# Holding the order of all five engines through the planned slots of a fused attention and mixture-of-experts kernel

## The chip, the cores and the metric

The kernel runs on one core of one Trainium2 chip. The metric is the device time of one launch in microseconds, as the median of three runs. One more execution was taken with the hardware profiler; the views quoted below are of that one.

## The reference, cut to what matters

Windowed attention with four sink positions gives the tokens `x`. A gate picks one of eight experts for each token, and that expert's two-layer network is applied to it.

```python
batch, n_heads, seq, head_dim = (4, 8, 768, 64); n_sink, window = (4, 128)
scores = scale * np.matmul(q, k.transpose(0, 1, 3, 2))
keep = is_sink | in_window
scores = np.where(keep, scores, -1000000000.0)
a = softmax(scores)                       # exp, sum + 1e-9
attn_out = np.matmul(a, v)
x = attn_out.transpose(0, 2, 1, 3).reshape(3072, 512)

logits = x @ w_gate                       # 8 experts
e_idx = np.argmax(logits, axis=1)
for e in range(8):
    mask = e_idx == e
    h = np.maximum(x[mask] @ w1[e], 0.0)  # 512 -> 1024
    ye = h @ w2[e]                        # 1024 -> 512
    out[mask] = gate_w[mask, None] * eom[mask, e, None] * ye
```

## The kernel before, in words

**Two stages.** The first stage runs attention over 16 pairs of heads, writes the tokens to `xd` in DRAM, and routes them. The second stage runs the experts' products over a fixed plan of 17 slots, numbered here k = 0 to 16. Slots 0 to 3 are the experts with most tokens, 256 rows each, known early. Slots 4 to 16 follow `SEQ` and `SIZES`: they hold 6, 1, 6, 2, 4, 1, 4, 2, 4, 1, 4, 2 and 1 units of 64 rows, so their products have m = 3, 3, 2, 2, 2 and 2 tiles of 128 rows, three have m = 1, and four are half tiles of 64 rows. Slot 16 is computed only when a flag asks for it.

**A slot.** "first(k)" is the product with w1 and "second(k)" the product with w2. Slots 0 and 1 use the weights as loaded (`plain1`, `plain2`, L576 and L589), as half slots do (`half1`, `half2`, L676 and L690). The others split each fp32 matrix into two fp32r halves and take three matmuls for one: `mm1_parts` (L545), `single_parts` for m = 1 (L601), `mm2_parts` (L650).

**Weights.** Each matrix comes in four pieces of 512 KB. A piece is loaded into one of four `raw` buffers (L486, on SP's queue), ACT casts it to the high half (L496), and POOL (pieces 0 and 2) or DVE (pieces 1 and 3) subtracts to get the low half (L497). Thirteen places a0 to a3, b0 to b2, c0 to c5 hold the halves; a place comes free when the product that reads it is done. In w1 a piece is one of the four depth blocks, and `mm1_parts` needs all four for its first output block; in w2 a piece serves two of the eight steps f.

**Tokens.** `gather` (L509) issues an indirect DMA on POOL into `xg`. `x_parts` (L519) copies the row factor (L524), transposes on PE (L527), casts on ACT to `xh` (L529) and subtracts on DVE to `xl` (L530), one tile of 128 rows at a time. After each first product `split_relu` (L535) makes `hh` on ACT and `hl` on DVE. `relu_transpose` (L593) is the way for m = 1 and half slots: DVE makes `hr` (L595), PE turns it (L598). `put` (L640) scales on ACT (L642) and scatters with an indirect DMA on POOL (L643).

**What sets the order.** Up to the end of slot 1 everything is emitted inside `tc.manual_schedule` with all five engines (L1060), so each engine runs its instructions as the program writes them. Routing work that is still open ("later": `gate_route`, `final_table`) is emitted in pieces by `points(3)` between the products of slots 0 and 1 (the "lane", L1017). From slot 2 on, only PE is held (the last loop of the second stage); the orders of ACT, DVE, POOL and SP come from the planner, which simulates the program by its own costs. There, weights are asked for up to three products ahead and the planner sets their casts, subtractions and loads where it finds room; the tiles of `x` are transposed in the second half of the product before.

Of the kernel before, what the change touches and what calls it, by code (L numbers as in the profile page):

```python
# [18 lines left out]
P = 128  # L19
# [30 lines left out]
CW = P + 4  # L50


def moe_kernel(tc, qT, kx, vx, vs, wgo, w1, w2, nsink, window, out):
# [7 lines left out]
    with ctx:  # L61
# [400 lines left out]
        def load_weights(which, ereg, slot, whole=False, parts=False):  # L462
# [6 lines left out]
            for i in range(4):  # L469
                view = src[bass.ds(ereg, 1), :, i * kk:(i + 1) * kk, :].rearrange("o p k n -> p (o k) n")  # L470
                if whole:
                    if i % 2 == 0:
                        pool, name = slot()
                    hi = pool.tile([P, kk, n], F32, name=name + "hl"[i % 2])
                    if parts:
                        loads.append(lambda hi=hi, view=view: nc.sync.dma_start(out=hi, in_=view))
                    else:
                        nc.sync.dma_start(out=hi, in_=view)
                    his += [hi[:, j, :] for j in range(kk)]
# [113 lines left out]
        def relu_transpose(mp, ps):  # L593
            hr = mp.tile([P, 4, P], F32, name="hr", bufs=2)
            nc.vector.tensor_scalar(out=hr, in0=ps.rearrange("p (a b) -> p a b", b=P), scalar1=0.0, scalar2=None, op0=ALU.max)  # L595
            tp = ps_t.tile([P, 4, P], F32, name="tp")
# [4 lines left out]
        def single_parts(mp, w, xs, hs):  # L601
# [12 lines left out]
            def turn(q):  # L614
                tp = relu_transpose(mp, both[:, q, :])
# [60 lines left out]
        def half1(mp, w, xf, hs):  # L676
# [28 lines left out]

        mctx = ctx.enter_context(ExitStack())
        ws = {}
        aa, bb, cc = (["%s%d" % (c, i) for i in range(n)] for c, n in (("a", 4), ("b", 3), ("c", NB)))
        second = iter(bb + aa[:1])
# [7 lines left out]
        with ExitStack() as actx:  # L717
# [201 lines left out]
            def early_rank(r):  # L919
                yield from rank_experts(*firsts(r))  # L920
                r0, n = firsts(r)
                for k in range(r0, min(r0 + n, 3)):
                    ws["e%d" % k] = expert_reg(order_i[0:1, k:k + 1])
                    for j in range(2) if k != 1 else ():
                        ws[k, j], loads, splits = load_weights(j, ws["e%d" % k], slot, whole=k == 0, parts=True)
                        if k == 0:
                            behind.extend(loads)
                        else:
                            stream.extend(zip(loads, splits))
                for load, _ in stream[:RAW]:  # L930
                    load()

            def second_weights(j):
                def name():
                    s = next(second)
# [3 lines left out]
            stream, at = [], [0]  # L939

            def weights():
# [429 lines left out]
```

## Time and profile before

| | |
|---|---|
| median of three runs | 574.55 us (572.3 to 582.35) |
| the profiled execution's own time | 581.05 us |
| its span, first to last instruction | 579.3 us |
| mean granted TensorE clock | 0.965 |
| busy: PE, PE weight load | 520.4 us (90%), 393.8 us (68%) |
| busy: DVE, ACT, POOL | 316.8 us (55%), 271.1 us (47%), 308.7 us (53%) |
| HBM read and written | 98.28 MB, 13.45 MB |

Engines: PE is the matmul engine, PEld its weight loads, DVE the vector engine, ACT the scalar engine, POOL GpSimd, SP the queue that issues most DMAs. A row of groups gives line, engine, operation, output and input tiles, shape and count, then total busy time and the mean of one in ns, then the idle time just ahead of the group and what ended it. A row of a timeline gives start, duration, the instruction, and in brackets the wait ahead of it and what ended that wait. A row of windows gives a stretch, its length, the busy time of PE, PEld, DVE, ACT and POOL in it, the granted clock, the DMA engines' busy share and GB/s. In the profiled execution attention ends and the lane begins near 185 us, first(2) starts at 259, the last product ends at 566.

### The profile page before, as it was taken

The numbers are of one execution on the slowest core, as the hardware profiler recorded it, in microseconds if no ns is written. First come the engines' busy times: TensorE is split into PE (matmuls) and PEld (weight loads), VectorE is DVE, ScalarE is ACT, GpSimd is POOL, SyncE is SP. The second block draws the span as 40 slices with busy tenths as digits, with TensorE's granted clock in tenths as the row PEclk, the third lists the DMA queues.
The fourth block names the chain that finished last, engine by engine and source line by source line (L and its number), as shares of the span: only waits on it lengthen the run. The fifth ranks groups of instructions, "written<-read, shape, count | busy, mean of one in ns | idle before, by whom it ended". The sixth has DMA issues, their size and how long they took to land. (4 is left out here: it accounts for less than half of the span.)

```text
span 579.3 us, 10514 instructions
## 1 busy us (share of the span) xinstructions
PE 520.4 (90%) x3432; PEld 393.8 (68%) x3432; DVE 316.8 (55%) x734; ACT 271.1 (47%) x721; POOL 308.7 (53%) x330
## 2 busy tenths in 40 slices
PE   3899999999888979987997999899999899997990
PEld 1566656656565845837896967788777787876870
DVE  5567699698777676982524151342454354553420
ACT  2576666666656122424524254343446354463310
POOL 4557757857856312636626344734466663666210
PEclk9999999999989979997999899999999899998996
DMA  6166776677996986348459645713998739977530
GB/s 228 61 137 185 153 156 166 130 147 209 215 238 102 226 225 165 110 150 286 147 174 360 230 133 193 240 46 126 365 334 270 237 128 320 369 249 242 183 135 19
DMA packets 72498, 112.85 MB, mean 195 GB/s; under 512 B 12044, under 2 KB 38672, under 8 KB 72434
## 3 DMA queue, kind: packets, MB, share of 16 engines
q1 hardware_dynamic: 67970, 98.16, 57.6%
q0 software_dynamic: 4464, 13.91, 6.9%
q8 instruction: 30, 0.49, 0.4%
q14 instruction: 34, 0.28, 0.2%
HBM read 98.28 MB, written 13.45 MB: 193 GB/s over the span
## 5 line engine op out<-in xcount | busy, mean ns | idle before, releaser
L788 ACT ACTIVATE e<-s,nmx 128x132 f32<-128x132 f32 x192 | 69.5, 367 | 66.5 <-DVE nmx L786 55.1
L776 PE MATMUL s<-kr,qr 64*128 64x260 f32 (+1 forms) x384 | 63.2, 429 | 16.2 <-ACT e L788 10.6
L537 DVE SCALAR_TENSOR_TENSOR hl<-s,hh 128x512 fp32r<-128x512 f32 (+1 forms) x32 | 24.0, 755 | 72.2 <-ACT hh L536 72.2
L776 PEld LDWEIGHTS s<-kr,qr 64*128 64x128 f32 x384 | 30.8, 199 | 40.3 <-ACT e L788 29.0
L643 POOL DMA_INDIRECT out_dram<-y,idx x20 | 23.6, 1182 | 48.2 <-ACT y L642 15.4
L536 ACT ACTIVATE hh<-s 128x512 fp32r<-128x512 f32 (+1 forms) x32 | 20.8, 650 | 54.0 <-PE s L556 53.9
L786 DVE TENSOR_REDUCE nmx<-s 128x2 f32<-128x264 f32 x96 | 41.5, 433 | 3.3
L763 POOL TENSOR_SCALAR qr<-qr 128x256 f32<-128x256 f32 x48 | 39.8, 848 | 1.1 <-DMA qr<-in_qT_dram 1.1
L83 POOL TENSOR_SCALAR_AFFINE_SELECT g<-f 128x512 f32<-128x512 f32 (+1 forms) x48 | 28.2, 588 | 21.3 <-DVE f L805 18.7
L788 ACT ACTIVATION_READ_ACCUMULATOR e<-s,nmx 128x1 f32 x192 | 37.6, 196 | 0.0
L782 DVE COPY_PREDICATED s<-maskf,s 128x256 f32<-128x256 int32 x80 | 33.7, 421 | 6.5 <-PE s L776 5.2
L509 POOL DMA_INDIRECT xg<-xd,idx x21 | 27.9, 1327 | 8.8 <-PE tp L527 4.9
L799 PE MATMUL tp<-ident,e 128*128 128x128 f32 x192 | 29.8, 295 | 0.4 <-ACT f L803 0.4
L799 PEld LDWEIGHTS tp<-ident,e 128*128 128x128 f32 x192 | 21.8, 148 | 11.8 <-issue 5.0
L83 POOL TENSOR_SCALAR_AFFINE_SELECT f<-f 128x512 f32<-128x512 f32 (+1 forms) x48 | 27.0, 562 | 3.3
L846 PE MATMUL oA<-f,vt 128*64 128x128 f32 x256 | 26.5, 285 | 0.4
L530 DVE TENSOR_TENSOR xl<-tp,xh 128x512 fp32r<-128x512 f32 x21 | 13.9, 683 | 17.5 <-ACT xh L529 17.5
L274 POOL TENSOR_TENSOR rhs<-oh,ohj 128x512 bf16<-128x512 bf16 x8 | 11.2, 1417 | 21.0 <-DVE oh L265 21.0
L643 POOL DMA_INDIRECT out_dram<-y,idx_e x8 | 8.7, 1084 | 23.7 <-ACT y L642 12.6
L803 ACT COPY f<-tp 128x512 f32<-128x512 f32 x32 | 18.6, 583 | 0.4 <-PE tp L799 0.4
L846 PE MATMUL oA<-g,vt 128*64 128x128 f32 x192 | 18.6, 273 | 0.0
L846 PEld LDWEIGHTS oA<-f,vt 128*64 128x64 f32 x256 | 14.4, 136 | 6.1 <-issue 3.3
(609 smaller groups left out, 1593.3 us busy)
## 6 DMA issues: line engine op xcount, KB each, us to landing
raw<-in_w_dram SPq DMA_DIRECT2D x88, 512.0 KB
kr<-in_kx_dram SPq DMA_DIRECT2D x16, 396.0 KB
qr<-in_qT_dram SPq DMA_DIRECT2D x16, 384.0 KB
vt<-in_vx_dram SPq DMA_DIRECT2D x16, 384.0 KB
xd<-x SPq DMA_DIRECT2D x16, 384.0 KB
a0h<-in_w_dram SPq DMA_DIRECT2D x4, 512.0 KB
a0l<-in_w_dram SPq DMA_DIRECT2D x4, 512.0 KB
b0h<-in_w_dram SPq DMA_DIRECT2D x3, 512.0 KB
```

Source lines behind the costliest of these rows:

```text
L83: nc.gpsimd.affine_select(out=ap, in_=ap if src is None else src, pattern=pattern, compare_op=op, fill=fill, base=base, channel_multiplier=cm)
L509: nc.gpsimd.indirect_dma_start(out=xg, out_offset=None, in_=xd[0:n + 1, :], in_offset=bass.IndirectOffsetOnAxis(ap=ids[0], axis=0))
L536: nc.scalar.activation(out=hi, in_=ps, func=AF.Relu)
L537: nc.vector.scalar_tensor_tensor(out=lo, in0=ps, scalar=0.0, in1=hi.bitcast(F32), op0=ALU.max, op1=ALU.subtract)
L643: nc.gpsimd.indirect_dma_start(out=where, out_offset=bass.IndirectOffsetOnAxis(ap=ids, axis=0), in_=y, in_offset=None, bounds_check=rows - ...
L763: nc.gpsimd.tensor_scalar(out=q, in0=q, scalar1=SCALE, scalar2=None, op0=ALU.mult)
L776: nc.tensor.matmul(out=s[:, a, o0:P + CW], lhsT=z["q"][r, t * P:(t + 1) * P], rhs=z["k"][r, k0:k0 + P + CW - o0], start=True, stop=True)
L782: nc.vector.copy_predicated(out=both[:, :, 4:CW], mask=bc(maski[:, 1, 4:CW], 1, 2), data=s[:, :, 0:P])
L786: nc.vector.tensor_reduce(out=m, in_=both, axis=AX.X, op=ALU.max, negate=True)
L788: nc.scalar.activation(out=z["e"][:, t, a, :], in_=both[:, a, :], func=AF.Exp, bias=m[:, a:a + 1], scale=1.0, accum_out=z["rs"][:, t, a:a ...
L799: nc.tensor.transpose(out=tp[:, k, :], in_=z["e"][:, 2 * j + k // 2, k % 2, 4:CW], identity=ident)
L846: nc.tensor.matmul(out=o, lhsT=v[:, kt, r], rhs=src[:, kt, a, :], start=t == kt == 0 or t == kt + 1 == 4, stop=False, skip_group_check=True)
```

## The change

All of the second stage moves into the region in which every engine is held. The routing pieces and slots 0 to 15 become one lane, each of whose steps is a piece of a product with a cost in microseconds; a running clock `now` adds these costs up, and `free` notes when a place comes free by that clock.

After each step `supply` may set one more piece of weights into the program: a split (cast and subtraction, followed by the next raw load), or for a half slot a load straight into its place. It does so when the place has been free for `LAG`, when `PACE` has passed since the last one, and when the raw load was issued at least `LAND` ago, all by `now`. `ensure` sets whatever is still missing directly ahead of the product that needs it.

The transposes of the next slot's `x` are set by the same clock, some microseconds ahead of the end of the product before. `hr` is emitted right behind the product that it reads, and turned later. The third tile of m = 3 goes to a tile of `s` rather than `oB`. One plain step of slot 0 moves ahead of the routing's counting matmuls, and the two tiles of `x` of slot 2 move from f = 6 of slot 1 to f = 3 and f = 5. The number of products, splits, loads, gathers and scatters is the same.

```diff
+LAG, PACE, LAND = 0.7, 1.7, 5.0
...
-                    hi = pool.tile([P, kk, n], F32, name=name + "hl"[i % 2])
+
+                    def straight(pool=pool, name=name, i=i, view=view):
+                        hi = (pool or pools[name[0]]).tile([P, kk, n], F32, name=name + "hl"[i % 2])
+                        nc.sync.dma_start(out=hi, in_=view)
+                        his.extend(hi[:, j, :] for j in range(kk))
+
...
-        def relu_transpose(mp, ps):
+        def relu(mp, ps):
             hr = mp.tile([P, 4, P], F32, name="hr", bufs=2)
             nc.vector.tensor_scalar(out=hr, in0=ps.rearrange("p (a b) -> p a b", b=P), scalar1=0.0, scalar2=None, op0=ALU.max)
+            return hr
+
+        def turned(hr):
             tp = ps_t.tile([P, 4, P], F32, name="tp")
             for f in range(4):
...
             products(0, range(2))
             yield
             products(0, range(2, ND))
+            h0 = relu(mp, both[:, 0, :])
             yield
-            products(1, range(2))
+            products(1, range(3))
             yield
-            turn(0)
-            products(1, range(2, ND))
+            turn(h0)
+            products(1, range(3, ND))
+            h1 = relu(mp, both[:, 1, :])
             yield
-            turn(1)
+            turn(h1)
...
-                ys = {s: ps_o.tile([P, DM], F32, name="oB" if s else "oA") for s in part}
+                ys = {s: s_tile()[:, 0, :] if part == [2] else ps_o.tile([P, DM], F32, name=("oA", "oB")[s]) for s in part}
...
+                if d == ND - 1:
+                    hr = relu(mp, ps)
                 yield
-            tp = relu_transpose(mp, ps)
+            tp = turned(hr)
             hf = mp.tile([P, 4, P], F32, name="hr", bufs=2)
...
+        steps = []
+        for k in range(2, n):
+            if not plan[k][2]:
+                steps.append(("first", k))
+            if k + 1 < n and plan[k + 1][2]:
+                steps.append(("first", k + 1))
+            steps.append(("second", k))
...
+            todo = [(k, 0 if f == "first" else 1) for f, k in steps] + [(len(plan) - 1, 0), (len(plan) - 1, 1)]
+            items, raws, names, free = [], [], {(0, 0): aa[:2], (0, 1): aa[2:], (1, 0): bb[:2], (1, 1): bb[2:] + aa[:1]}, {}
...
+            now, put_at, n_put, n_raw = [0.0], [0.0], [0], [0, 0]
+            def build():
+                if not todo or todo[0][0] >= NE and later:
+                    return False
+                k, w = todo.pop(0)
...
+                half = plan[k][2]
+                ws[k, w], loads, splits = load_weights(w, ws["e%d" % k], named, half, True)
+                for i in range(4):
+                    x = dict(key=(k, w), name=used[i // 2 if half else i], again=half and i % 2 == 1, load=loads[i],
+                             split=None if half else splits[i])
+                    items.append(x)
+                    if not half:
+                        raws.append(x)
+                return True
+            def feed():
+
+                while n_raw[0] < n_raw[1] + RAW:
+                    if n_raw[0] == len(raws):
+                        if not build():
+                            return
+                        continue
+                    x = raws[n_raw[0]]
+                    x["load"]()
+                    x["at"] = now[0]
+                    n_raw[0] += 1
+
+            def place():
+                x = items[n_put[0]]
+                n_put[0] += 1
+                assert x["again"] or free.get(x["name"], 0) is not None
+                free[x["name"]] = None
+                if x["split"] is None:
+                    x["load"]()
+                else:
+                    if "at" not in x:
+                        feed()
+                    x["split"]()
+                    n_raw[1] += 1
+                    feed()
+                put_at[0] = now[0]
+
+            def supply():
+                if n_put[0] == len(items) and not build():
+                    return
+                x = items[n_put[0]]
+                at = free.get(x["name"], 0)
+                if (x["again"] or at is not None and at <= now[0] - LAG) and now[0] >= put_at[0] + PACE:
+                    if x["split"] is None or x.get("at", now[0]) <= now[0] - LAND:
+                        place()
+
+            def ensure(key):
+                while not all(x["key"] != key for x in items[n_put[0]:]) or key in todo:
+                    if n_put[0] == len(items):
+                        while later:
+                            point()
+                        assert build()
+                    place()
+
+            def lane_step(on=False):
+
+                x = next(lane, None)
+                if x is None:
+                    return False
+                cost, done = x
+                now[0] += cost
+                for key, i in done:
+                    free[names[key][i]] = now[0]
+                if on:
+                    supply()
+                return True
...
                         if (i - NP, g) < (1, 1):
-                            next(lane)
+                            lane_step()
                         points(3)
-                        if (i - NP, g) < (1, 1):
-                            next(lane)
+                        if (i - NP, g) != (1, 1):
+                            lane_step()
...
+                    xg2 = xgs[k + 1] = early_gather(k + 1)
+                    ys = outs()
+                    for f in range(NF):
+                        if k == 0 and f == 6:
+                            xf = plain_x(mx, xg2)
+                        if k == 1:
+                            if f == 3:
+                                xs[2] = []
+                                g = x_parts(mx, xg2, xs[2])
+                            if f in (3, 5):
+                                next(g)
+                        plain2(ws[k, 1], h, ys, f)
+                        yield 1.75, [((k, 1), f // 4)] if f % 4 == 3 else []
...
+            def rows_of(k):
+                ids = plan[k][1]
+                while later and k >= NE:
+                    point()
+                for j in range(max(k, NE), min(k + AHEAD, len(plan))):
+                    if j not in there and not later:
+                        there.add(j)
+                        load_ids(plan[j][3])
+                xgs[k] = early_gather(k) if k < NE else [gather(mx, a) for a in ids]
...
+            def first(k):
+                hs[k] = []
+                m = len(xgs[k])
+                if plan[k][2]:
+                    parts, size, cost, last = half1(mp, ws[k, 0], xs[k][0], hs[k]), 4, 0.9, range(2)
+                elif m > 1:
+                    parts, size, cost, last = mm1_parts(mp, ws[k, 0], xs[k], m, range(0, NF, 2), hs[k]), 8, 0.7 * m, range(4)
+                else:
+                    parts, size, cost, last = single_parts(mp, ws[k, 0], xs[k], hs[k]), 4, 1.4, range(4)
+                return parts, [(cost, []) for _ in range(size - 1)] + [(cost, [((k, 0), i) for i in last])]
+
+            def second(k):
+                ids, half = plan[k][1:3]
+                if half:
+                    return (half2(mp, ws[k, 1], hs[k], xgs[k][0], ids[0]),
+                            [(0.9, [((k, 1), f // 2)] if f % 2 else []) for f in range(4)])
+                m = len(xgs[k])
+                costs = [(0.7 * min(m, 2), [((k, 1), f // 2)] if f % 2 else []) for f in range(NF)]
+                return mm2_parts(mp, ws[k, 1], hs[k], xgs[k], ids), [(0.7, [])] * NF * (m == 3) + costs
+
+            def slots():
+
+
+                rest = None
+                for i, (f, k) in enumerate(steps):
+                    ensure((k, 0 if f == "first" else 1))
+                    parts, costs = first(k) if f == "first" else second(k)
+                    whole = sum(c for c, _ in costs)
+                    tasks = []
+                    if rest is not None:
+                        tasks.append((1.2, rest))
+                        rest = None
+                    j = queue[0]
+                    follows = steps[i + 1:i + 3]
+                    x = None
+                    if plan[j][2]:
+                        if j < len(plan) - 1 and f == "first" and follows[0] == ("first", j):
+                            x = to_x(j)
+                    elif f == "second" and ("first", j) in follows and not plan[k][2]:
+                        x = to_x(j)
+                    if x is not None:
+                        m = len(xgs[j])
+                        end = whole - (0 if follows[0] != ("first", j) else 2.4)
+                        tasks += [(max(0.1, end - 1.5 * (m - a)), x) for a in range(m)]
+                    tasks.sort(key=lambda z: z[0])
+                    t = 0.0
+                    for n, (c, done) in enumerate(costs):
+                        next(parts)
+                        t += c
+                        for _ in range(2):
+                            if tasks and tasks[0][0] <= t:
+                                next(tasks.pop(0)[1], None)
+                        yield c, done
+                    for z in tasks:
+                        next(z[1], None)
+                    if f == "first" and len(xgs[k]) == 1:
+                        rest = parts
+                    else:
+                        assert next(parts, None) is None
+                    if x is not None:
+                        assert next(x, None) is None
+                        queue.pop(0)
+                        rows_of(queue[0])
+                while n_put[0] < len(items) or todo:
+                    if n_put[0] == len(items):
+                        assert build()
+                    place()
...
-                for i, _ in enumerate(lane):
-                    if i in (1, 4) or 8 <= i < 20 and i % 2 == 0:
-                        weights()
+                while lane_step(True):
                     points(3)
-            while at[0] < len(stream):
-                weights()
...
-            rows_of(queue[0])
-            with tc.manual_schedule(engines={ET.PE}):
-                for i, (f, k) in enumerate(steps):
-                    for x in loads[i:i + 3]:
-                        fetch(*x)
-                    parts = f(k)
-                    size = 4 if f is first and len(xgs[k]) == 1 or plan[k][2] else 8
-                    if f is second and len(xgs[k]) == 3:
-                        size = 16
-                    x = None
-                    if (steps + [(None, n)])[i + 1][0] is first:
-                        x = to_x(queue[0])
-                    late = f is first and len(xgs[k]) == 1
-                    for c in range(size):
-                        next(parts)
-                        if rest is not None and c == (1 if size == 8 else 0):
-                            assert next(rest, None) is None
-                            rest = None
-                        if x is not None and c >= size // 2 - 1:
-                            next(x, None)
-                    if x is not None:
-                        assert next(x, None) is None
-                        queue.pop(0)
-                        rows_of(queue[0])
-                    if late:
-                        rest = parts
-                    else:
-                        assert next(parts, None) is None
```

More of the change, by code (lines that the diff above doesn't have):

```diff
@@ L703, in expert_reg, with load_ids @@
             return nc.sync.value_load(ap, min_val=0, max_val=E - 1)
+        plan = [(order_i[0:1, r:r + 1], [(idx_e[:, 0, r, j:j + 1], idx_e[:, 1, r, j:j + 1]) for j in range(2)], False) for r in range(NE)]
+        for q in SEQ:
+            cols = [[idx[:, q, i, j:j + 1] for j in range(3)] for i in range(-(-SIZES[q] // 2))]
+            plan.append((exp_i[0:1, q:q + 1], cols, SIZES[q] == 1, q))
+        n = len(plan) - 1
+        steps = []
[5 more added lines that the diff above has]
+            steps.append(("second", k))
+        queue = [k for f, k in steps if f == "first" and k > 2] + [n]
+        there = set()
+        def load_ids(q):
+            at = nc.sync.value_load(lin_i[0:1, q:q + 1], min_val=0, max_val=(E - 1) * NJP + NJ)
+            z = SIZES[q]
+            for a in range(2):
+                r = slice(a * U, (a + 1) * U)
+                if z == 1:
+                    src = unitd[:, bass.ds(at, 1), :]
+                    nc.sync.dma_start(out=idx[r, q, 0:1, 0:2], in_=src[:, :, 0:2])
+                    nc.sync.dma_start(out=idx[r, q, 0:1, 2:3], in_=src[:, :, 2 + a:3 + a])
+                else:
+                    src = unitd[:, bass.ds(at, z), :].rearrange("u (i a) c -> u i a c", a=2)
+                    nc.sync.dma_start(out=idx[r, q, 0:z // 2, 0:2], in_=src[:, :, a, 0:2])
         mctx = ctx.enter_context(ExitStack())
@@ L923, in early_rank @@
                     ws["e%d" % k] = expert_reg(order_i[0:1, k:k + 1])
[L924 to L927, printed above, removed]
-                        else:
-                            stream.extend(zip(loads, splits))
-                for load, _ in stream[:RAW]:
-                    load()
+                    for j in range(2) if k == 0 else ():
+                        ws[k, j], loads, _ = load_weights(j, ws["e%d" % k], slot, whole=True, parts=True)
+                        behind.extend(loads)
@@ L1017, in early_slots @@
             def early_slots():
-                ids = ws["ids"] = [[(idx_e[:, 0, r, j:j + 1], idx_e[:, 1, r, j:j + 1]) for j in range(2)] for r in range(NE)]
                 def outs():
@@ L1040, in early_slots @@
[L1040 to L1052 removed]
+                        put(mp, ys[s], xg[s][1], DM, out, NTOK, plan[k][1][s][1])
@@ L1235, in fetch @@
-            def fetch(k, which):
-                if (k, which) not in ws:
-                    if which == 0:
-                        ws["e%d" % k] = expert_reg(plan[k][0])
-                    ws[k, which] = load_weights(which, ws["e%d" % k], slot, plan[k][2])
-            xgs, xs, hs = {2: ws["xg"]}, {2: ws["xs"]}, {}
-            n = len(plan) - 1
-            def rows_of(k):
-                ids = plan[k][1]
-                for j in range(max(k, NE), min(k + AHEAD, len(plan))):
-                    if j not in there:
-                        there.add(j)
-                        load_ids(plan[j][3])
-                xgs[k] = early_gather(k) if k < NE else [gather(mx, a) for a in ids]
@@ L1267, in second @@
-            def second(k):
-                ids, half = plan[k][1:3]
-                if half:
-                    return half2(mp, ws[k, 1], hs[k], xgs[k][0], ids[0])
-                return mm2_parts(mp, ws[k, 1], hs[k], xgs[k], ids)
-            ahead = [k for k in range(2, n) if plan[k][2]]
-            steps = []
-            for k in range(2, n):
-                if k not in ahead:
-                    steps.append((first, k))
-                if k + 1 in ahead:
-                    steps.append((first, k + 1))
-                steps.append((second, k))
```

130 lines of the change are left out of this document (49 added, 81 removed).

## The prediction

> **What bounds the kernel now.** I read the page's head first, then the windows by stage.
>
> ```profile
> span 579.3 us, 10514 instructions
> PE 520.4 (90%) x3432; PEld 393.8 (68%) x3432; DVE 316.8 (55%) x734; ACT 271.1 (47%) x721; POOL 308.7 (53%) x330
> ```
>
> ```profile
> 185.00:567.00 382.00, 356.86 (x1932) 0.96 0.65 214
> ```
>
> ```profile
> 259.20:264.30 5.10, 0.60 (x2) 0.31 (x2) 2.94 (x3) 1.61 (x3) 4.51 (x4) 0.81 0.81 257
> ...
> 314.80:318.10 3.30, 0.08 (x1) 0.08 (x1) 3.17 (x2) 0.57 (x1) 3.14 (x2) 0.83 1.04 375
> ...
> 450.40:453.40 3.00, 0.50 (x4) 0.29 (x2) 2.84 (x3) 1.78 (x3) 2.54 (x3) 1.00 0.60 214
> ...
> 525.20:528.90 3.70, 0.65 (x4) 0.34 (x2) 3.04 (x3) 2.79 (x5) 3.24 (x3) 0.96 0.67 228
> ...
> 566.30:579.30 13.00, 0.00 (x0) 0.00 (x0) 0.00 (x0) 0.69 (x1) 0.98 (x1) 0.62 0.07 20
> ```
>
> PE is the bound. From 185 to 567, where the change lies, it idles 382.0 - 356.9 = 25.1 us, and 4.5 + 3.2 + 2.5 + 3.1 = 13.3 of these lie in four holes, each ahead of a first product: first(2), first(4), first(8), first(12). PE's waits by cause say what ends them:
>
> ```profile
> PE s L556 <- ACT xh L529: 7.3, 4, 4.5
> PE s L556 <- DVE xl L530: 7.0, 4, 3.2
> ...
> PE tp L598 <- DVE hr L595: 3.4, 4, 1.0
> ```
>
> Always the transposed `x`, never a weight. The engines' own timelines show why `xh` and `xl` are late:
>
> ```profile
> 450.06 1.07 ACT L529 CAST xh<-tp 128x512 fp32r<-128x512 f32 x2
> ...
> 524.57 1.04 ACT L496 CAST c1h<-raw 128x1024 fp32r<-128x1024 f32 x1 [1.22 <-DMA raw<-in_w_dram]
> 525.52 1.07 ACT L529 CAST xh<-tp 128x512 fp32r<-128x512 f32 x2
> ```
>
> ```profile
> 313.57 3.80 DVE L497 TENSOR_TENSOR a0l<-raw,a0h 128x1024 fp32r<-128x1024 f32 x1 [1.21 <-ACT a0h L496]
> 317.29 0.68 DVE L530 TENSOR_TENSOR xl<-tp,xh 128x512 fp32r<-128x512 f32 x1
> ```
>
> The planner put splits ahead of them: ACT stands waiting for a raw load while `xh` is next in its queue, and DVE finishes a subtraction before the last `xl`. A hole also costs clock behind it:
>
> ```profile
> 263.50:269.20 5.70, 5.50 (x24) 5.21 (x25) 1.92 (x2) 3.43 (x6) 3.65 (x3) 0.50 0.99 345
> 269.20:272.00 2.80, 2.80 (x26) 2.80 (x26) 0.69 (x1) 0.60 (x1) 2.00 (x1) 1.00 0.91 288
> ...
> 318.00:323.60 5.60, 5.58 (x17) 5.58 (x18) 0.00 (x0) 0.19 (x1) 1.23 (x2) 0.50 1.02 401
> ...
> 453.30:457.20 3.90, 3.90 (x20) 3.90 (x21) 0.00 (x0) 0.47 (x1) 3.59 (x3) 0.56 1.04 334
> ...
> 528.70:532.60 3.90, 3.85 (x20) 3.85 (x21) 0.00 (x0) 0.23 (x1) 3.39 (x2) 0.58 0.87 222
> ```
>
> Behind each hole the granted clock (third column from the right) is half for 4 to 6 us: lost 5.6 x 0.50 = 2.8 behind the second, 3.9 x 0.44 = 1.7 and 3.9 x 0.42 = 1.6 behind the last two. At full clock 26 matmuls take 2.80 us, 0.108 each.
>
> **Gains: x set by the clock.** The transposes of slot 4 now come at 5.6, 7.0 and 8.4 of second(3)'s 11.2 planned us (tasks at 4.3, 5.8, 7.3, taken at the next 1.4 us piece), and by the diff's own sums only loads without a cast are set in that stretch: hole and clock go, 3.2 + 2.8 = 6.0. Slots 8 and 12 get theirs at the start of second(7) and second(11), with 3 us and more to spare, so the hole ahead of first(8), 2.5 + 1.7 = 4.2, and that ahead of first(12) as far as `x` causes it, 3.1 + 1.6 = 4.7, go too. Of the 14.3 us that PE waits for `xh` and `xl`, 1.0 lies elsewhere (14.3 - 4.5 - 3.2 - 2.5 - 3.1), and goes. `hr` is now emitted nine matmuls or a planned 1.2 us ahead of its turning, more than its wait of 1.0 at most: 3.4 goes. Together 19.3. Cover: if a split still stands ahead of an `x` tile, one cast (1.05) or one POOL subtraction (2.4, below) comes back per product.
>
> **No gain: the first hole.** Here the casts moved earlier don't help, since DVE is late itself:
>
> ```profile
> 221.20:257.40 36.20, 36.20 (x129) 22.94 (x128) 33.00 (x136) 11.78 (x17) 12.04 (x8) 1.00 0.47 130
> ```
>
> ```profile
> 258.65 2.20 DVE L497 TENSOR_TENSOR b0l<-raw,b0h 128x1024 fp32r<-128x1024 f32 x1 [1.27 <-ACT b0h L496]
> ...
> 263.53 0.69 DVE L530 TENSOR_TENSOR xl<-tp,xh 128x512 fp32r<-128x512 f32 x1 [2.08 <-ACT xh L529]
> ```
>
> DVE works through the routing's last pieces from 221.2 to 257.4 almost without a gap, long behind their emission, and the moved `xl` stand behind all of them. The change takes away the 1.3 + 2.1 of waiting on ACT, and sets one more DVE subtraction (b2l, 1.2) and up to two more POOL ones (2.4 each, which stop DVE, see a0l above: 1.2 alone, 3.8 there) ahead of the last `xl`: between 264.2 - 3.4 + 1.2 = 262.0 and 266.8. The plain step that moves ahead of the counting matmuls only makes PE arrive earlier and wait longer. I take 264, no gain, with -2 and +3 as ends. The Trainium skill (SBUF — State Buffer, "SBUF: two separate sides") states that VectorE and GpSimd share a port pair as an exclusive lock, held for a whole instruction; by that rule both POOL subtractions count in full, the hole ends at 266.8, 2.6 us later than before, and the forecast would be 580. The row of a0l agrees with the rule.
>
> **Costs: splits that come too late.** `supply` is asked once per piece and keeps `PACE` = 1.7. So pieces of 1.4 let one split through every 2.8 planned us, pieces of 0.7 one every 2.1, and the loads of half slots use up turns as well. Added up by the diff's costs: from the start of second(10) to first(12), 22.4 us, eleven splits are due (three pieces of slot 11's w1, four of its w2, four of slot 12's w1) and eight get a turn (four in second(10), two in first(11), two in second(11)). `ensure` sets one ahead of second(11) and two, pieces 2 and 3, directly ahead of first(12). Before first(14) four loads take second(12)'s turns, and again pieces 2 and 3 are left. The same happens with some time to spare ahead of second(12), second(14) and second(15), since there a piece serves only two of eight steps. In the held order these splits stand behind the previous product's `put`, and `mm1_parts` needs them after eight matmuls. Prices:
>
> ```profile
> L642 ACT ACTIVATE y<-oA,sc 128x512 f32<-128x512 f32 x13 | 8.9, 687 | 11.8 <-PE oA L661 7.0 <-PEq L1321 3.0 <-PE oA L591 1.9
> L643 POOL DMA_INDIRECT out_dram<-y,idx x20 | 23.6, 1182 | 48.2 <-ACT y L642 15.4 <-ACTq L1321 9.3 <-DMA b1h<-in_w_dram 5.4
> L509 POOL DMA_INDIRECT xg<-xd,idx x21 | 27.9, 1327 | 8.8 <-PE tp L527 4.9 <-issue 2.5 <-PE tp L672 0.5
> L496 ACT CAST a2h<-raw 128x1024 fp32r<-128x1024 f32 x7 | 7.3, 1047 | 6.2 <-PE oB L591 5.1 <-DMA raw<-in_w_dram 0.6 <-PE oA L696 0.4
> L497 POOL TENSOR_TENSOR b0l<-raw,b0h 128x1024 fp32r<-128x1024 f32 x2 | 4.8, 2400 | 10.1 <-ACT b0h L496 9.5 <-DMA raw<-in_w_dram 0.6
> ```
>
> first(12): from PE's last matmul of second(11), scaling 0.69, scatter 1.18, gather of slot 13 1.33, subtraction on POOL 2.40: 5.6, less eight matmuls (0.9): 4.7, and 2.8 of clock: 7.5. The low end, with POOL out of the way, is scaling, two casts and a DVE subtraction of 1.23: 4.0 - 0.9 = 3.1.
>
> first(14): POOL starts behind second(12) with scaling, two scatters, a gather and piece 0's subtraction, 0.69 + 2.36 + 1.33 + 2.40 = 6.8; then the half slot's scatter and piece 2's subtraction, 10.4. PE has second(13) for cover,
>
> ```profile
> 338.00:341.50 3.50, 3.50 (x17) 1.01 (x16) 2.83 (x2) 2.96 (x4) 3.04 (x2) 1.00 0.37 122
> ```
>
> 3.5 us by the like half product here, and eight matmuls: 6.0 of waiting, 8.8 with clock.
>
> Small ones: two tiles of `x` (slots 8 and 12) are turned soon after their gathers, which queue on POOL behind two scatters:
>
> ```profile
> xg<-xd,idx POOLq DMA_INDIRECT x21, 4.1
> ```
>
> 0.69 + 2.36 + 1.33 + 4.1 = 8.5 for the second tile's landing, and 7.2 for the first, against a first product of 5.6 and one step of 0.7: about 1.0 each. second(15), pieces 2 and 3 of five with POOL and DVE in turn: 2. second(12), piece 0 on POOL: 1. Together 5, between 0 and 9. Sum of costs 7.5 + 8.8 + 5 = 21.3.
>
> **Nothing:** the third tile of m = 3 on `s` removes a wait for `oB` that PE's waits don't show. On SP the loads of token ids and expert numbers for slot 4 on, which wait for DVE's routing, now stand behind all raw loads of slots 2 and 3, and only loads for slot 4 on are queued behind them, 30 us ahead of their use; uncovered, a raw load would come about 5 us later. Raw loads see no new wait: the plan issues each raw at least 5.6 us ahead of its cast, nearly always over 8, and slot 16's loads need no place that is freed late. The tail of 13 us stays.
>
> **Sum.** 581.05 - 19.3 + 0 + 21.3 = 583 for a profiled execution like this one. That execution stands 1.011 above the median of 574.55; scaled, 583.05 / 1.011 = 576.5. I forecast 577: no change. About 2% (563 to 586) is what a measurement of this kernel can tell from none.
>
> **Rivals.** *Late splits hidden*: ACT and POOL run ahead of PE, as they do in the trace before (never a wait for a weight), and the two big waits shrink below what trips the clock, to 1 each, the small ones to 2. For it: POOL is 53% busy. Against: the held order puts them behind a scaling that needs PE's last matmul. Then -19.3 + 4 = -15.3, about 559. Chance 0.26.
> *POOL's queue cascades*: where two slots' scatters, gathers and subtractions meet, from first(11) on, each raw buffer waits for its POOL subtraction, so the next raw load, the next cast and the next product shift too. It decides once a subtraction ends over 5 us behind its cast, since that is all that `LAND` leaves. Then second(12), second(14), first(15) and second(15) each lose 3.1 (first(12)'s low end) and 1.6 of clock: 4 x 4.7 = 18.8 less the small costs of 3 counted there, 577 + 16 = 593. Chance 0.22.
> *The change doesn't do what it says*: the planner's order was much the same, holes stay, no split comes late: 574.5. Chance 0.04.
>
> **How the numbers follow.** The forecast has 0.48: 19.3 may be 15 to 20, the costs 14 to 26, the first hole -2 to +3, so 567 to 587 for itself. Faster by over 2%: the first rival and a little of the forecast, 0.27; slower: 0.25; same: 0.48. The range takes in both rivals' likely halves: 558 to 592.
>
> **What would show it.** Right: no hole ahead of first(4) and first(8), no wait of L598 on `hr`; new holes of 4 to 7 us ahead of first(12) and first(14), ended by a POOL or DVE subtraction L497, half clock behind them; the hole ahead of first(2) at least as long and still ended by `xl`. Wrong: PE never waiting for L497, or first(2) starting before 260.

## The result and the profile after

The change made the kernel slower: 610.5 us (median of 4 runs, 609.4 to 613.7) against 573.4 (571.5 to 582.4) beside it, a ratio of 1.060 with a 95% interval of 1.054 to 1.067. The forecast of 577 and its range, 558 to 592, were wrong. The profiled execution of after took 610.17, 29.1 us more than that of before.

The head of after's page, then its windows by stage (columns as in before's: PE, weight loads, VectorE, ACT and POOL busy, granted clock, DMA share, GB/s):

```profile
span 608.4 us, 10491 instructions
PE 521.0 (86%) x3432; PEld 393.6 (65%) x3432; DVE 325.5 (54%) x734; ACT 269.0 (44%) x721; POOL 302.4 (50%) x330
```

```profile
185.00:595.20 410.20, 358.53 (x1935) 286.00 (x1933) 187.50 (x339) 154.44 (x237) 179.38 (x110) 0.94 0.61 200
248.10:259.90 11.80, 0.03 (x1) 0.00 (x0) 10.88 (x38) 3.63 (x4) 7.54 (x4) 0.59 0.58 189
317.50:319.50 2.00, 2.00 (x11) 1.77 (x11) 0.00 (x0) 1.46 (x3) 2.00 (x1) 1.00 0.04 16
...
413.50:420.00 6.50, 5.36 (x24) 4.60 (x25) 1.95 (x4) 2.55 (x7) 0.00 (x0) 0.74 0.08 31
...
501.30:505.40 4.10, 0.20 (x2) 0.00 (x0) 1.23 (x1) 0.59 (x1) 3.72 (x3) 0.68 0.76 242
505.40:509.00 3.60, 3.60 (x17) 3.60 (x18) 0.00 (x0) 0.00 (x0) 1.93 (x2) 0.50 1.01 318
```

PE does the same work, 521 us, and idles 410.2 - 358.5 = 51.7 us where before idled 25.1. The hole ahead of first(4) is gone (317.5 to 319.5 is full, at full clock). New holes stand at 248, 409, 488, 502, 540 and 581. PE's waits by cause name other partners than before's `xh` and `xl`:

```profile
PE tp L532 <- DMA xg<-xd,idx_e: 11.8, 1, 11.8
...
PE tp L532 <- DMA xg<-xd,idx: 9.1, 2, 5.5
PE oA L671 <- POOL c2l L502: 5.8, 1, 5.8
...
PE s L561 <- POOL c3l L502: 5.1, 1, 5.1
PE s L561 <- POOL b0l L502: 3.9, 1, 3.9
```

They are gathers that land late and subtractions on POOL that end late. The table gives each product's length from the timeline of PE, from the start of its first matmul to the end of its last (a row with an arrow: from start to start). "After again" is a second profile of the same kernel; the other columns are the experiments below.

| us | before | after | after again | e1 | e2 | e4 | e7 | e6 | e11 |
|---|---|---|---|---|---|---|---|---|---|
| second(1) -> second(2) | 33.5 | 39.8 | 33.4 | 33.0 | 33.2 | 33.4 | 36.1 | 32.9 | 36.1 |
| first(4) | 23.6 | 17.5 | 17.5 | 17.5 | 17.5 | 17.4 | 17.4 | 17.5 | 17.4 |
| second(7) | 7.1 | 14.1 | 15.4 | 14.7 | 7.1 | 7.1 | 7.2 | 9.7 | 12.3 |
| second(8) -> first(10) | 17.9 | 17.2 | 17.2 | 21.8 | 17.2 | 23.0 | 16.3 | 17.4 | 17.1 |
| second(11) | 7.1 | 12.6 | 14.0 | 17.6 | 9.6 | 7.7 | 7.6 | 10.9 | 15.2 |
| first(12) | 13.1 | 19.5 | 19.5 | 13.2 | 18.7 | 12.1 | 12.1 | 12.2 | 13.3 |
| first(14) | 15.1 | 22.6 | 22.8 | 12.1 | 21.9 | 11.8 | 13.3 | 11.6 | 11.7 |
| second(15) | 6.2 | 14.3 | 14.3 | 6.7 | 17.3 | 6.7 | 6.7 | 6.2 | 6.2 |

**Why the gathers are late.** POOL's timeline in after, between second(6) and second(7) (start, duration, instruction, idle time before it):

```profile
401.70 1.00 POOL L653 DMA_INDIRECT out_dram<-y,idx  x1 [2.79 <-ACT y L652]
406.63 0.98 POOL L653 DMA_INDIRECT out_dram<-y,idx  x1 [3.93 <-issue]
407.92 0.99 POOL L514 DMA_INDIRECT xg<-xd,idx  x1 [0.30 <-PE tp L606]
409.22 0.97 POOL L514 DMA_INDIRECT xg<-xd,idx  x1 [0.30 <-issue]
```

```profile
414.64 1.09 PE L532 MATMUL tp<-ident,xg 128*128 128x128 f32 x4 [5.51 <-DMA xg<-xd,idx]
```

The two scatters of `put` write the same output, and the second starts 4.9 us after the first, though the first's own row is 1.00 long. The profile gives no cause in this row; the like pair behind second(10), ahead of the gathers of slot 12, has it:

```profile
481.22 1.00 POOL L653 DMA_INDIRECT out_dram<-y,idx  x1
486.51 0.98 POOL L653 DMA_INDIRECT out_dram<-y,idx  x1 [4.28 <-DMA out_dram<-y,idx]
```

The second waits until the first has landed. The Trainium skill (Perfetto Trace Analysis, "DMA Instruction — SWDGE (GPSIMD)") states that the profiled end of such an instruction is the end of descriptor writing and not of the data's move; the 1.00 beside the 4.9 agrees. It isn't the queue that is slow: a gather behind a scatter starts 0.30 us after that scatter's row. Behind both scatters stand the gathers of slot 8, whose tile PE wants one step into second(7). The gather itself is late too: from its row's start (407.92) to PE's turning (414.64) it takes 6.7 us, for slot 12 only 3.4 (487.80 to 491.20). The DMA engines were busier in the first stretch (share 0.88 against 0.63); whether that is the reason was not tried.

**Why the subtractions are late.** The same queue ahead of first(14), and PE's two stops:

```profile
535.68 1.02 POOL L653 DMA_INDIRECT out_dram<-y,idx  x1 [10.72 <-ACT y L652]
540.30 1.01 POOL L653 DMA_INDIRECT out_dram<-y,idx  x1 [3.61 <-ACT y L652]
541.62 0.99 POOL L514 DMA_INDIRECT xg<-xd,idx  x1 [0.30 <-issue]
542.63 2.35 POOL L502 TENSOR_TENSOR c3l<-raw,c3h 128x1024 fp32r<-128x1024 f32 x1
545.15 1.81 POOL L653 DMA_INDIRECT out_dram<-y,idx  x1 [0.17 <-issue]
546.97 2.37 POOL L502 TENSOR_TENSOR c5l<-raw,c5h 128x1024 fp32r<-128x1024 f32 x1
```

```profile
545.03 0.58 PE L561 MATMUL s<-xh,c3l 128*128 128x256 f32 x1 [5.06 <-POOL c3l L502]
549.39 0.58 PE L561 MATMUL s<-xh,c5l 128*128 128x256 f32 x1 [2.71 <-POOL c5l L502]
```

The weights' splits were emitted behind `put`, scatter and gather, and POOL holds that order. For the scatter at 540.30 the profile names ACT's `y`, but the `y` that it writes was done at 536.15 on ACT's timeline; that it too waits for the first scatter's landing is inferred from the pairs above.

### The profile page after: what moved, and what is told of

It is laid out like the page before. It is cut to its first block, busy times and chain, and to the rows that moved or that the text cites. A ratio compares the mean times of both kernels' runs of the same rounds, so it can differ in the third digit from the quotient of the medians.

```text
span 608.4 us, 10491 instructions
## 1 busy us (share of the span) xinstructions
PE 521.0 (86%) x3432; PEld 393.6 (65%) x3432; DVE 325.5 (54%) x734; ACT 269.0 (44%) x721; POOL 302.4 (50%) x330
## 5 line engine op out<-in xcount | busy, mean ns | idle before, releaser
L819 PE MATMUL s<-kr,qr 64*128 64x260 f32 (+1 forms) x384 | 63.4, 431 | 17.1 <-ACT e L831 11.4
L653 POOL DMA_INDIRECT out_dram<-y,idx x20 | 25.1, 1256 | 48.7 <-ACT y L652 23.0
L532 PE MATMUL tp<-ident,xg 128*128 128x128 f32 x84 | 14.2, 296 | 20.9 <-DMA xg<-xd,idx_e 11.8
L534 ACT CAST xh<-tp 128x512 fp32r<-128x512 f32 x21 | 12.3, 587 | 41.2 <-PE tp L532 41.2
L532 PEld LDWEIGHTS tp<-ident,xg 128*128 128x128 f32 x84 | 10.9, 151 | 25.8 <-DMA xg<-xd,idx_e 12.6
L514 POOL DMA_INDIRECT xg<-xd,idx x21 | 24.6, 1173 | 5.9 <-issue 4.0
L502 POOL TENSOR_TENSOR c0l<-raw,c0h 128x1024 fp32r<-128x1024 f32 x4 | 9.7, 2430 | 23.7 <-ACT c0h L501 23.7
L652 ACT ACTIVATE y<-oA,sc 128x512 f32<-128x512 f32 (+1 forms) x16 | 10.4, 650 | 23.4 <-DMA out_dram<-y,idx 9.3
```

Source lines behind the costliest of these rows:

```text
L514: nc.gpsimd.indirect_dma_start(out=xg, out_offset=None, in_=xd[0:n + 1, :], in_offset=bass.IndirectOffsetOnAxis(ap=ids[0], axis=0))
L532: nc.tensor.transpose(out=tp[:, d, :], in_=xg[:, d * P:(d + 1) * P], identity=ident)
L653: nc.gpsimd.indirect_dma_start(out=where, out_offset=bass.IndirectOffsetOnAxis(ap=ids, axis=0), in_=y, in_offset=None, bounds_check=rows - ...
L819: nc.tensor.matmul(out=s[:, a, o0:P + CW], lhsT=z["q"][r, t * P:(t + 1) * P], rhs=z["k"][r, k0:k0 + P + CW - o0], start=True, stop=True)
```

## The experiments

Theory: what costs time is POOL's and ACT's held order, with the splits left to the last moment and the gathers behind scatters that wait for one another. Rivals: POOL is simply full; the positions are wrong in any order; VectorE is late in any case. Each ratio is to the kernel before on the same chip (before's median there was 581.5 for e0 to e3, 582.7 for e4 to e7 and 576.6 for e8 to e11); intervals are 95%.

**e0_before_again**: the kernel before, unchanged.

> The kernel before once more, for a second profile of it. The profiled execution of before took 581 us, its other runs 571 to 575. Theory: the difference of some 7 us lies in its holes ahead of first products and the half clock behind them (first(2), first(4), first(10), first(14)), and this execution, near 574, has shorter or fewer of them. Rival: it lies in the attention part ahead of 185 us.

It took 580.9 once more, with the same waits (`xl` 7.6, `xh` 7.4), so neither side of that expectation was tested. What follows is that the profiled 581 of before was no outlier: over the sets its runs lie between 571 and 589.

**e1_pace**: no split left to be forced.

```
-LAG, PACE, LAND = 0.7, 1.7, 5.0
+LAG, PACE, LAND = 0.7, 1.3, 5.0
```

> After, with PACE 1.3 in place of 1.7: every piece of 1.4 planned us may take a split, and by the diff's own sums none is left to be forced ahead of first(12), first(14) or second(15). Theory (these holes are the forced splits alone): first(12) 19.5 to 12, first(14) 22.6 to 12, second(15) 14.3 to 7, together about -25 us, 585. Rival (POOL's queue is full there, whatever the pace): the splits come earlier in the order, but scatters and gathers now stand behind them, the holes move and at most 8 us come back, 602 or more.

591.2 us, ratio 1.022 (1.012 to 1.033). first(12), first(14) and second(15) lose 6.3, 10.5 and 7.6 us, as the theory had it, and the time is well under the rival's 602. But the rival was right that holes move; other waits grow:

```profile
PE tp L532 <- DMA xg<-xd,idx: 13.9, 2, 8.3
PE oA L708 <- ACT y L652: 6.8, 3, 3.7
```

The wait for slot 12's gather goes from 3.6 to 8.3 (9.1 for slots 8 and 12 together before this edit): its two scatters start 6.5 us apart here, 5.3 in after, and the gather lands 6.4 us after its start, 3.4 in after. Half slots wait longer for a scaling on ACT. About 10 of 24 us are given back.

**e2_gather_first**: in `slots`, the next slot's gathers go ahead of the previous product's `put`; `sc` gets more buffers for it (8 in e4 and the runs built on it).

```
-name="sc", bufs=6
+name="sc", bufs=12
...
+if x is not None:
+    assert next(x, None) is None
+    queue.pop(0)
+    rows_of(queue[0])
 if f == "first" and len(xgs[k]) == 1: rest = parts
 else: assert next(parts, None) is None
-if x is not None: ... rows_of(queue[0])
```

> After, with the next slot's gathers emitted ahead of the previous product's scalings and scatters instead of behind them. Theory (second(7) and second(11) wait because the gather of slots 8 and 12 stands on POOL behind two scatters, the second of which waits about 4 us for the first one's landing): second(7) 14.1 to 7.5 and second(11) 12.6 to 7.5, -11 us, 599. Rival (the tiles are turned too early for any gather: the transposes stand one step into a product of 5.6 us): half of both waits stays, 605.

604.5 us, ratio 1.046 (1.035 to 1.058). POOL's timeline at the same place:

```profile
392.99 1.00 POOL L514 DMA_INDIRECT xg<-xd,idx  x1
394.30 1.84 POOL L514 DMA_INDIRECT xg<-xd,idx  x1 [0.30 <-issue]
396.45 1.02 POOL L653 DMA_INDIRECT out_dram<-y,idx  x1 [0.30 <-issue]
401.36 1.00 POOL L653 DMA_INDIRECT out_dram<-y,idx  x1 [3.90 <-DMA out_dram<-y,idx]
```

second(7) is back to 7.1 and second(11) to 9.6, and no wait for a gather of slots 8 or 12 is left: the rival (turned too early for any gather) falls. The scatters, and the splits behind them, now come later: second(15) grows from 14.3 to 17.3 and first(10) from 13.2 to 17.5, where PE waits 4.0 us for an `hl` of VectorE. So the total gain is less than the 10 us of the two products.

**e3_slot2**: slot 2's gather ahead of slot 1's first product.

```
 h = []
+if k == 1: xg2 = xgs[2] = early_gather(2)
 for f0 in range(0, NF, 2): ...
-xg2 = xgs[k + 1] = early_gather(k + 1)
+if k == 0: xg2 = xgs[1] = early_gather(1)
```

> After, with slot 2's gather emitted ahead of slot 1's first product instead of behind it, so ahead of the splits of that stretch on POOL. Theory (PE's 11.8 us in second(1) are the gather's place behind splits that wait for their raw loads): the hole ended by the gather's landing goes, first(2) starts at 262 to 264 in place of 270.9, -7 us, 603. Rival (the prediction's own step: VectorE is late with the last xl because of the routing, whatever the gather does): a hole of 3 to 5 us ahead of first(2), ended by xl, at 265 to 267, -4 us, 606. If the loads set the pace (casts of c5 and b0 wait for raw): first(2) no earlier than 268.

608.2 us, ratio 1.049 (1.038 to 1.060), not to be told from after. second(1) has no hole any more (14.8 long), but PE stops behind it:

```profile
PE s L561 <- DVE xl L535: 4.4, 1, 4.4
```

From second(1) to second(2) it took 34.1 us, before 33.5. So VectorE is what is late there, as the prediction's step and this run's rival say; its wait for `xl` ended at 265.9. VectorE's own timeline shows what lies ahead of the second `xl`:

```profile
259.00 1.23 DVE L502 TENSOR_TENSOR c4l<-raw,c4h 128x1024 fp32r<-128x1024 f32 x1
260.14 3.37 DVE L502 TENSOR_TENSOR b0l<-raw,b0h 128x1024 fp32r<-128x1024 f32 x1
263.44 0.68 DVE L535 TENSOR_TENSOR xl<-tp,xh 128x512 fp32r<-128x512 f32 x1
264.04 1.21 DVE L502 TENSOR_TENSOR b2l<-raw,b2h 128x1024 fp32r<-128x1024 f32 x1
265.17 0.68 DVE L535 TENSOR_TENSOR xl<-tp,xh 128x512 fp32r<-128x512 f32 x1
```

b0l took 3.37 instead of 1.2 while POOL's b1l ran (259.05 to 262.43). This is as the rule that the prediction weighed (the Trainium skill, SBUF — State Buffer, "SBUF: two separate sides") says. 265.9 is nearer to the 266.8 of that step than to the 264 that was taken, but the whole stretch is only 0.6 us longer than before's.

**e4_pace_gather**: e1 and e2 together.

> After, with PACE 1.3 and with the gathers ahead of the previous product's scalings and scatters. Theory (two separate causes, the forced splits and the gathers behind scatters): from 591 of PACE alone, second(7) 14.7 to 7.1 and second(11) 17.6 to 8, so 574, about the kernel before. Rival (POOL has no room for both): the scatters come later for the gathers, the half products' wait for a scaling (6.8 in all with PACE 1.3) doubles, 582 or more.

576.6 us, ratio 0.993 (0.988 to 0.997), near the theory's 574. Together the two edits take 6.7% off after's ratio, alone 3.8% and 1.4%: the causes are two, but not separate, since each edit alone lengthens the other's wait (17.6 for second(11) in e1, 17.3 for second(15) in e2). The rival is half right: the half slots' wait for a scaling rose from 6.8 to 9.5, but not to double.

**e5_y3**: e4 with `bufs=3` for `y`; a table that isn't used on this path (`io128`) is built elsewhere to make room (from here on, the runs built on e5 have each line of the code one line higher: L531 is L532 of after).

> The same as e4_pace_gather with three y tiles instead of two (a table of the path that doesn't run here is built where it is used, to make room). Theory (ACT stands in its held order at a scaling that waits for a scatter's landing, with casts and relus behind it, and the half products wait for oA): the half products' waits of 0.8, 3.7 and 2.3 us with PACE 1.3 fall under 1 in all, and with their half clock 6 to 8 us go: 567. Rival (the second scatter waits on POOL for the first's landing in any case, and the scaling is late for a cast that waits for its raw load): under 2 us.

575.0 us, ratio 0.990 (0.983 to 0.997), and that wait is 9.2: the theory fails. ACT's timeline shows the rival at work, a cast for a later slot that waits for its raw load, ahead of the scaling:

```profile
437.00 1.04 ACT L500 CAST a0h<-raw 128x1024 fp32r<-128x1024 f32 x1 [1.30 <-DMA raw<-in_w_dram]
...
438.52 1.05 ACT L500 CAST a1h<-raw 128x1024 fp32r<-128x1024 f32 x1
439.47 0.69 ACT L651 ACTIVATE y<-oA,sc 128x512 f32<-128x512 f32 x1
```

second(8) had ended at 436.4; its scaling comes 3.1 us later, and PE starts the half product at 440.2.

**e6_pe_only**: after, with the order of TensorE alone held from slot 2 on; the other engines' comes from the planner, as in before.

```
-while lane_step(True): points(3)
+while not began and lane_step(True): points(3)   # began: set as slots() starts
+with tc.manual_schedule(engines={ET.PE}):
+    while lane_step(True): points(3)
```

> After, with only TensorE's order held from slot 2 on; ACT, VectorE, GpSimd and SyncE in the order that the framework gives, as in before; the positions of the splits, loads and gathers in the program as in after. Theory (the loss is the held order of POOL and ACT): gathers and scatters are no longer held one behind the other, second(7) and second(11) come back to 7 or 8, and the forced splits at first(12), first(14) and second(15) lose part of their wait: 580 to 592. Rival (the positions alone: a split emitted late is late in any order): 603 or more.

590.6 us (582.6 to 594.7), ratio 1.016 (1.010 to 1.023) against after's 1.060. No wait for a subtraction of POOL is left, at the old PACE, with each split at the same place in the program. POOL's timeline ahead of first(14):

```profile
526.00 1.78 POOL L514 DMA_INDIRECT xg<-xd,idx  x1
528.11 1.02 POOL L653 DMA_INDIRECT out_dram<-y,idx  x1 [0.32 <-ACT y L652]
529.55 2.37 POOL L502 TENSOR_TENSOR c0l<-raw,c0h 128x1024 fp32r<-128x1024 f32 x1 [0.43 <-ACT c0h L501]
534.78 1.01 POOL L653 DMA_INDIRECT out_dram<-y,idx  x1 [2.85 <-PE s L561]
```

The planner sets a gather ahead of the scatter, and a subtraction between two scatters. The rival (positions alone) is out: PE waits for the late subtractions only where the order is held. What is left against before lies in other holes: first(3) takes 16.3 (11.5 in after), where `xh` and `xl` come late, and second(11) 10.9.

**e7_y3_half2**: e5, and the half slots' second product on another tile.

```
-ys = ps_o.tile([P, DM], F32, name="oA")
+ys = s_tile()[:, 0, :]
```

> The same as e5_y3 with the half slots' second product on an s tile instead of oA, so that it doesn't wait for the previous product's scaling. Theory (with three y tiles the scaling is in time): no more than 1 us, 567. Rival (the scaling is late for the casts ahead of it on ACT): the half products' waits go here and not in e5_y3, 3 to 6 us faster than e5_y3.

567.1 us, ratio 0.977 (0.969 to 0.985): the rival was right, the half products' wait goes here (second(8) to first(10): 21.9 in e5, 16.3 here), and the gain of 8 us is more than its 3 to 6. This version is faster than both kernels; whether by 2% of before, the interval leaves open. PE is busy 90% of a span of 565.3 again, and what is left is slot 2's gather and small waits:

```profile
PE tp L531 <- DMA xg<-xd,idx_e: 7.8, 1, 7.8
PE s L618 <- DVE hr L599: 3.0, 3, 1.4
```

**e8_after_again**: after, unchanged.

> After once more, unchanged, for a second profile. Theory (slot 2's gather stands behind the subtraction c5l, and that behind a raw load whose wait was 6.1 us in after's profile and 2.0 with PACE 1.3, with the same order up to there): second(1) differs from one execution to the next, 22 here in place of 28.7; the rest as before, 603 to 611. Rival (the first profile is typical): 28 to 29.

609.0 us, ratio 1.057 (1.050 to 1.063). second(1) took 21.9 this time, with 5.2 us of waiting for slot 2's gather in place of 11.8; the other lengths repeat to 1.7 us. The gather's place explains part of the spread. ACT and POOL in after:

```profile
249.43 1.04 ACT L501 CAST c5h<-raw 128x1024 fp32r<-128x1024 f32 x1 [6.12 <-DMA raw<-in_w_dram]
```

```profile
250.55 2.35 POOL L502 TENSOR_TENSOR c5l<-raw,c5h 128x1024 fp32r<-128x1024 f32 x1 [7.03 <-ACT c5h L501]
253.05 1.87 POOL L514 DMA_INDIRECT xg<-xd,idx_e  x1
```

The gather stands behind c5l, c5l behind its cast, and the cast waited 6.1 us for a raw load in after, 2.4 in this run and 2.0 in e1. That is 3.7 of the 6.6 us. The other 2.9 are the gather's landing: from its row's start to PE's turning 6.9 us in after (253.05 to 259.93) and 4.0 here (252.53 to 256.54). Why either takes so different a time was not tried.

**e9_slot2_too**: e7 with e3's edit.

> The same as e7_y3_half2 with slot 2's gather ahead of slot 1's first product too. From second(1) to the end of first(2) e7_y3_half2 took 36.3 us, the run with that gather alone 34.3, and PACE alone 33.1. Theory (VectorE is late with the last xl in any case): no gain that can be measured, 0 to -2 us, and the wait is put down to xl. Rival (the gather is what is late): -4 to -8 us.

568.2 us, ratio 0.984 (0.977 to 0.991): no gain to be seen against e7's 0.977, as in e3, and again `xl` 4.4 and `xh` 1.8.

**e10_hr_back**: e7 with the single slots' relu back at its turning, `products(1, range(2))` ahead of it.

> The same as e7_y3_half2 with the relu of the single slots back in front of its turning, and two of the second half's four products ahead of it, as in before. Theory (the change's earlier relu gained nothing, since the second half's products now wait for it on the same s tile, L619 2.4 us in three): first(7), first(11) and first(15) stay at 7.2 and the time is the same within 1 us. Rival (the prediction's 3.4 us): 3 us slower.

569.9 us, ratio 0.988 (0.982 to 0.994), 1.7 us from e9 on the same chip, and in this execution second(1) to second(2) alone was 5 us longer than in e9. first(7) and first(15) are 7.2 as in e7, but second(7) and second(11) are 1.5 and 2.0 longer, and PE waits 5.2 us for `hr` where it waited 3.2 in e7. From second(2) to the end e10 took 274.2 us, e9 274.3 and e7, on another chip, 269.5. So this run doesn't decide between theory and rival: the earlier relu can be worth 2 us or so in this order, and whether it shortens the kernel stays open.

**e11_pe_only_too**: e7 with TensorE's order alone held.

> The same as e7_y3_half2 with only TensorE's order held from slot 2 on. Theory (what was lost was lost to an order that put the wrong things ahead, and the mended order is as good as the framework's or better): 0 to +15 us against e7_y3_half2, since with TensorE alone held after kept holes at first(3), second(7), second(11). Rival (holding the order is a loss in itself): 4 us or more faster than e7_y3_half2.

589.9 us, ratio 1.021 (1.011 to 1.030), 4% slower than e7, more than the theory's 15 us allowed; the rival fails. Here the planner's order stands in the way: in second(11), 15.2 long, VectorE has a split for a later product ahead of the `hl` that PE needs next:

```profile
491.01 6.07 DVE L501 TENSOR_TENSOR a2l<-raw,a2h 128x1024 fp32r<-128x1024 f32 x1
497.00 0.41 DVE L627 TENSOR_TENSOR hl<-tp,hh 128x256 fp32r<-128x256 f32 x1
```

PE waits 5.4 us for that `hl`; two subtractions on POOL (491.3 to 496.0) stretch a2l from 1.2 to 6.07.

So to hold the order is neither a gain nor a loss by itself: in after it cost about 4% (e6 against after), in the mended order it is worth about 4%.

## Why the prediction was wrong, step by step

The prediction's sum for a profiled execution was 583; after's took 610.2, and after again 606.8. Its steps, against before's lengths (several of the signs that it named came true: no hole ahead of first(4), new ones in first(12) and first(14) that end with a subtraction, half clock behind them):

- **x set by the clock.** Right for first(4): 6.0 forecast, 6.1 measured. The other two holes it named stand ahead of first(10) and first(14), not of first(8) and first(12) as the text has it: the products counted through PE's timeline put them there. The gain came all the same, since `x` of slots 10 and 14 is now turned in second(8) and second(12): from the half product to the end of first(10) 4.4 us less (4.2 forecast); first(14) with what lies ahead of it came out 5.1 longer, and -4.7 + 8.8 = 4.1 was forecast.
- **hr, 3.4.** Failed. The wait moved: the second half's products write the same `s` tile and now wait for the relu ("PE s L619", 2.4 in three, and 0.8 at L606). first(7), first(11) and first(15) became 0.6 us longer together: 4.0 off.
- **No gain: the first hole.** VectorE is late by itself, as e3 and e9 show, and the size was right in after again (33.4 against 33.5) and in e1, e2, e4. But that was luck: the hole was to be ended by `xl` still, and it is ended by the gather. With POOL's order held that stands behind a subtraction that waits for a raw load, and in the profiled execution it cost 6.3.
- **first(12) and first(14).** The mechanism held, and the sizes nearly: first(12) 7.5 longer by the forecast and 6.4 by the trace, first(14) as just told; second(12) 1 and 1.4. For first(14) the size is partly luck: from second(12)'s end to c5l's end POOL took 14.0 us and not 10.4, since the second scatter came 4.6 after the first, and PE waited 7.8 and not 6.0.
- **Small ones, 5 us.** This is the term that failed. The two tiles of `x` were priced at 1.0 each and cost 7.0 and 5.5. Their price holds 2.36 for two scatters on POOL, and from the first's start to the second's end these take 5.9 (401.70 to 407.61) and 6.3 (481.22 to 487.49), because the second waits for the first's landing: the duration of a row was taken for the time in which its queue moves on. By the sum the first tile lands 7.2 us behind the second product before; PE could turn it 13.3 behind second(6) and 11.5 behind second(10). The scatters are 3.5 and 3.9 of these 6.1 and 4.3 us; for slot 8 another 2.6 is the gather's landing, 6.7 where 4.1 was taken. second(15) was priced at 2, for subtractions in turn, and cost 8.1: its first subtraction, c2l, ended at 587.0 behind a scatter that had waited 4.9 us behind the one before it. (For that wait the profile names ACT's `hh`, which the scatter doesn't use.) A hole then costs clock as well (0.50 from 505.4 to 509.0).
- **The scale of 1.011.** It took 6 us off; after's profiled execution stands at its own median (610.2 and 610.5), so for after there was nothing to take off.

The price of the scatters was in before's profile. The view from which the gather's 4.1 was read has the scatter's landing in its next row:

```profile
out_dram<-y,idx POOLq DMA_INDIRECT x20, 6.8
```

And in before's POOL timeline, from 265 us on, no scatter starts less than 3.5 us after another; the pairs at 403 and 481 us are 6.5 and 6.3 apart.

Together 4.0 + 6.3 + 10.5 + 6.1 = 26.9 of the 27 us between 583 and 610.2. The rest about cancels; one part of it, 2.6 us ahead of second(5) for a scaling on ACT, the sum doesn't have. Of the rivals, "POOL's queue cascades" was nearest (593), but not by its mechanism: it took 4.7 us each from second(12), second(14), first(15) and second(15), and these grew by 1.4, 0, 0.4 and 8.1; it needed raw buffers held by subtractions, and e1 shows that the late splits' places were at fault. "Late splits hidden" fell.

## What to carry to other kernels

Where an order is fixed by hand on an in-order queue, price each entry by when the next one may start, not by its own row: a store that the next store must wait for costs its landing, so what the next product needs (gathers, splits) goes ahead of it. Holding an order pays only when that order has been read through engine by engine; the same positions were 4% better left to the planner, and the mended ones 4% better held. A pace that the step doesn't divide (1.7 against 1.4) halves the rate, and what is left over comes due at once.

## What was not expected of the hardware

A second indirect store to the same output started 4.6 to 5.3 us after the first in each pair shown above (535.68 and 540.30; 401.70 and 406.63; 481.22 and 486.51; 396.45 and 401.36), for rows of 1.0 us. And in two executions of the same kernel one raw load kept its cast waiting 6.1 and 2.4 us, and one gather landed 6.9 and 4.0 us after its start, at the same places in the program; PE's wait there was 11.8 and 5.2.
